# Score matmuls over 64 rows in two row groups instead of 32 rows in four

## The chip, the cores and the metric

The kernel runs on one core of a Trainium2 chip. Five engines work side by side and meet through semaphores: TensorE (PE, matrix products into PSUM), VectorE (DVE), ScalarE (ACT), GpSimd (POOL) and SyncE (SP, which issues the transfers). The metric is the time of one execution on the device in microseconds; less is better. Before the change two executions gave a median of 1937.16 us (1934.91 to 1939.40).

## The reference, cut to what matters

One sequence of 2048 tokens with 512 features passes through four blocks, each with a residual: multi-query softmax attention (A), linear attention (B), A again, B again, with the same weights. Block A has 32 heads of 16 features and one key and one value head that all share. `B_x` isn't used.

```python
def _A_ref(x, wq, wk, wv, wo):
    H = 32; Dh = D // H                       # 16
    q = (x @ wq).reshape(B, S, H, Dh).transpose(0, 2, 1, 3)
    k = x @ wk                                # (B, S, 16): one key for all heads
    v = x @ wv
    scores = jnp.einsum("bhqd,bkd->bhqk", q, k) * (Dh ** -0.5)
    p = softmax(scores)
    o = jnp.einsum("bhqk,bkd->bhqd", p, v)
    return o.transpose(0, 2, 1, 3).reshape(B, S, H * Dh) @ wo

def _B_ref(x, wqkv, wo):                      # linear attention, 32 heads of 16
    q, k, v = split_heads(x @ wqkv)
    pq, pk = phi(q), phi(k)                   # phi(t) = (t + 1 if t > 0 else exp(t)) + 1e-6
    kv = jnp.einsum("bhsd,bhse->bhde", pk, v); z = pk.sum(2)
    o = (pq @ kv) / (pq @ z + 1e-6)
    return merge_heads(o) @ wo

for layer in range(2):
    x = x + _A_ref(_layernorm(x), ...)
    x = x + _B_ref(_layernorm(x), ...)
```

Almost all the work is the softmax attention: per layer 32 heads x 2048 queries x 2048 keys, each with one exponential.

## The kernel before

**Units and positions.** A layer's attention is cut into 4 query blocks of 512 tokens (qb), 4 groups of 8 heads (g) and two halves of a group (par): 32 units. A unit holds 4 heads, called j, and goes over 16 tiles of 128 keys (kt): 64 positions (kt, j), in that order, with j running fastest (`Ctl.start`, L541 to L551). Two layers have 4096 positions.

**Scores.** `QT` holds the queries of a group with their 8 x 16 features on the 128 partitions. Four row groups of 32 partitions hold two heads each. Keys of 16 features are repeated on all partitions and kept in two masked copies, `Kr[:, 0]` and `Kr[:, 1]` (L486 to L496): copy par has zeros in the 16 rows of the other head of each pair. A position's scores are one matmul, keys against 512 queries, contracted over the 32 rows of row group j with copy par (`smm`, L572); the zeros take the second head out.

**Two ways from scores to weights.** PSUM has eight banks of 512 columns. Banks 0 to 2 and 3 to 5 are two sets: `fill` (L668) puts three positions into a set, and ACT exponentiates all 1536 columns in one instruction into one of the `PTA` buffers (L689). Bank 6 takes single positions for DVE, which works the exponential out in seven steps: L735 for each position, and L751 to L756 for two positions at once, into a `PTD` buffer (`dstep`, `dpass`). DVE's positions are taken `LEAD` = 26 ahead of ACT's. The same bank 6 serves all other products while attention runs: projections, transposes, residuals.

**PV.** For each position four matmuls (L608) multiply 128 queries' weights with `Vaug` (16 value columns and a column of ones) into 17 columns of bank 7, which collects a unit's 16 blocks of (query tile, head). After 64 positions DVE takes the reciprocals of the sums (L620) and writes the scaled result into `Osb` (L625); then the bank is free for the next unit. When both halves of a group are done, `epi_tr` (L793) transposes `Osb`, and after four groups `epi_y` applies `wo` and the residual (L809).

**Dense work beside attention.** When a query block of tokens is finished, its layer norm, the projections of linear attention (`b_prep`, `kv_block`, phi at L815 to L818) and their sums run beside the attention of the next blocks. So block 0 of a layer has little of it, blocks 1 to 3 have some 80 dense matmuls of 512 columns each. After the last block `b_main` runs the 16 tiles of linear attention (L889 to L931) and, in layer one, starts the layer norms and key projections of layer two (`a_ready`): this is the ramp, in which attention starts with one set.

**The order.** `Sched` plays the whole program through once, when the kernel is built, with a planned duration for each operation (`dur`), a priority and the state of buffers and banks. The order in which it starts operations on each engine is the order that is written out; semaphores carry the dependencies. The engines don't reorder at run time. `Ctl.step` decides in this play when a set is filled and when DVE takes a position. Planned durations of the score matmuls (L684, L734) don't depend on rows.

The softmax here doesn't subtract the row's maximum and nothing guards it: scores larger than these inputs give would overflow.

## Time and profile before

| | |
|---|---|
| median of two executions | 1937.16 us (1934.91 to 1939.40) |
| the profiled execution | 1937.57 us, span 1935.7 us |
| mean granted TensorE clock | 0.575 |
| busy: PE, DVE, ACT | 1778.2, 1712.9, 1702.0 us |
| score matmuls L572 | 4096 |
| PV matmuls L608 | 16384 |
| dense matmuls L475 | 704 |
| exponentials on ACT L689 | 1179 of up to three positions |
| positions on DVE L735 | 560 |

The profile's page gives the busy time of each engine, a row of 40 equal slices of the span with the granted clock of TensorE in tenths (5 is half, 9 is 90% or more), and groups of instructions: line, engine, operation, what it writes and reads, count, busy time and mean duration, then the idle time before them and what ended it. PEld are the weight loads, which overlap the matmuls. In rows by stretch, each number is the busy time of PE, PEld, DVE, ACT and POOL in that stretch with the number of instructions, then the granted clock, the share of the transfers and GB/s. In rows in order of time, the numbers are start and length in us. The ends of matmuls are modelled, so two starts say more than one length.

### The profile page before, as it was taken

To read this page: it belongs to the slowest core of one execution; us is meant where nothing else is said; L and a number is where in the kernel's file an instruction comes from. 1 tells how busy PE (TensorE), PEld (TensorE's weight loads), DVE (VectorE), ACT (ScalarE), POOL (GpSimd) and SP (SyncE) were. 2 spreads that over 40 slices of the span, in tenths; PEclk is the share of its full clock that TensorE was granted. 3 is DMA by queue.
4 is the path that set the end of the run, shared out by engine and by line. 5 is a ranking of instruction groups with operands and counts; after the bars stand their busy time and mean duration, and the time that the engine had idled before them with its cause. 6 is when DMAs were issued, how large, how long until landed. Compare 5 with 4: busy or idle time off the path is not lost.

```text
span 1935.7 us, 49030 instructions
## 1 busy us (share of the span) xinstructions
PE 1778.2 (92%) x22208; PEld 820.9 (42%) x22208; DVE 1712.9 (88%) x3063; ACT 1702.0 (88%) x1330; POOL 45.1 (2%) x77
## 2 busy tenths in 40 slices
PE   7999999999999999998889999999999999997977
PEld 4444444444444444443444444444444444443434
DVE  7899989999889988887879999899898989985977
ACT  6999999999989999997589999999998999986973
POOL 2000000000000000000100000000000000000000
PEclk8555556555665555555975555655565555556559
DMA  3000000000000000000000000000000000000001
GB/s 110 2 1 2 2 1 2 2 2 2 1 2 2 2 1 2 2 2 2 1 2 2 2 2 2 2 2 2 1 2 1 2 1 2 2 2 1 2 1 44
DMA packets 7808, 10.50 MB, mean 5 GB/s; under 512 B 1456, under 2 KB 7088, under 8 KB 7600
## 3 DMA queue, kind: packets, MB, share of 16 engines
q1 hardware_dynamic: 7600, 7.37, 1.2%
q8 instruction: 173, 2.83, 0.6%
q14 instruction: 35, 0.29, 0.0%
HBM read 5.28 MB, written 2.10 MB: 4 GB/s over the span
## 4 chain that ended last, share of the span: by engine, by line
PE 57%; DVE 29%; ACT 11%; issue 1%; DMA 0%; POOL 0%; SPq 0%
PE ps_all L572 27%; PE ps_all L608 16%; PE ps_all L475 11%; ACT PTA L689 10%; DVE xT L735 8%; DVE PTD L756 6%; DVE xu L751 3%; DVE xs L755 2%; DVE xs L752 2%; DVE xu L754 1%; DVE xs L753 1%; PE ps_all L920 1%; DVE stats L444 1%; PE ps_all L458 1%; DVE x_sb L931 1%
## 5 line engine op out<-in xcount | busy, mean ns | idle before, releaser
L689 ACT ACTIVATE PTA<-ps_all 128x1536 bf16<-128x1536 f32 x1179 | 1625.1, 1464 | 117.7 <-PE ps_all L572 108.8
L572 PE MATMUL ps_all<-QT,Kr 32*128 32x512 bf16 x4096 | 914.0, 582 | 80.0 <-ACT PTA L689 38.8
L608 PEld LDWEIGHTS ps_all<-Vaug,PTA 128*128 128x128 bf16 x14144 | 470.3, 104 | 566.0 <-issue 552.6
L608 PE MATMUL ps_all<-Vaug,PTA 128*128 128x17 bf16 x14144 | 584.0, 176 | 4.6 <-ACT PTA L689 2.5
L735 DVE TENSOR_SCALAR xT<-ps_all 128x512 int32<-128x512 f32 x560 | 385.1, 688 | 116.1 <-PE ps_all L572 105.1
L756 DVE SCALAR_TENSOR_TENSOR PTD<-xT,xs 128x1024 uint16<-128x1024 int32 x280 | 340.5, 1216 | 1.1
L572 PEld LDWEIGHTS ps_all<-QT,Kr 32*128 32x128 bf16 x4096 | 160.0, 98 | 311.6 <-ACT PTA L689 152.6
L751 DVE TENSOR_SCALAR xu<-xT 128x1024 f16<-128x1024 uint16 x280 | 192.3, 687 | 3.1
L755 DVE TENSOR_TENSOR xs<-xs,xu 128x1024 f16<-128x1024 f16 x280 | 191.0, 682 | 1.4
L752 DVE TENSOR_TENSOR xs<-xu 128x1024 f16<-128x1024 f16 x280 | 190.4, 680 | 0.5
L608 PE MATMUL ps_all<-Vaug,PTD 128*128 128x17 bf16 x2240 | 111.6, 176 | 16.6 <-DVE Osb L625 8.0
L753 DVE TENSOR_SCALAR xs<-xs 128x1024 f16<-128x1024 f16 x280 | 116.4, 416 | 1.0
L754 DVE TENSOR_SCALAR xu<-xu 128x1024 f16<-128x1024 f16 x280 | 117.0, 418 | 0.0
L608 PEld LDWEIGHTS ps_all<-Vaug,PTD 128*128 128x128 bf16 x2240 | 86.1, 104 | 66.8 <-DVE Osb L625 26.9
L475 PE MATMUL ps_all<-wqkv_sb,xnT 128*128 128x512 bf16 x256 | 106.3, 559 | 2.6 <-ACT xnT L464 1.4
L448 POOL TENSOR_TENSOR rstd<-veps,mhalf 128x1 f32<-128x1 f32 x64 | 40.9, 643 | 1842.2 <-DVE veps L446 1623.6
L815 ACT ACTIVATE e_buf<-ps_all 128x512 f32<-128x512 f32 x64 | 37.8, 597 | 39.8 <-PE ps_all L475 38.7
L475 PE MATMUL ps_all<-xnT,wq_sb 128*128 128x512 bf16 x128 | 55.8, 566 | 4.4 <-DVE xT L735 2.1
L475 PE MATMUL ps_all<-xnT,wqkv_sb 128*128 128x512 bf16 x128 | 52.4, 545 | 6.5 <-DVE pqT L818 5.6
L475 PE MATMUL ps_all<-wo_sb,OT 128*128 128x512 bf16 x128 | 51.9, 543 | 2.9 <-ACT OT L799 1.4
L444 DVE BATCH_NORM_STATS2 stats<-x_sb 128x6 f32<-128x512 bf16 x64 | 43.2, 683 | 3.5 <-DMA x_sb<-in_A_x_dram 3.3
L458 PE MATMUL ps_all<-ident,xn_buf 128*128 128x128 bf16 x256 | 31.2, 267 | 15.3 <-DVE xn_buf L451 13.6
(64 smaller groups left out, 625.9 us busy)
## 6 DMA issues: line engine op xcount, KB each, us to landing
out_dram<-x_sb SPq DMA_DIRECT2D x16, 128.0 KB, 1.7
x_sb<-in_A_x_dram SPq DMA_DIRECT2D x3, 512.0 KB, 7.3
wqkv_sb<-in_B_wqkv_dram SPq DMA_DIRECT2D x1, 1536.0 KB, 11.3
x_sb<-in_A_x_dram SPq DMA_DIRECT2D x2, 256.0 KB, 3.5
wq_sb<-in_A_wq_dram SPq DMA_DIRECT2D x1, 512.0 KB, 5.5
wo_sb<-in_A_wo_dram SPq DMA_DIRECT2D x1, 512.0 KB, 8.5
wo_sb<-in_B_wo_dram SPq DMA_DIRECT2D x1, 512.0 KB, 10.9
wk_sb<-in_A_wk_dram SPq DMA_DIRECT2D x1, 16.0 KB, 2.7
```

Source lines behind the costliest of these rows:

```text
L444: add(DV, tdv(512), lambda e: e.bn_stats(stats[:, t, 0:6], x_sb[:, t, :]), reads=[("x", t)], writes=[("st", t)], prio=prio, name="bn")
L475: i = e.matmul(bank(h.idx, n), lhsT=l, rhs=r, start=(c + k == 0), stop=(c + k == len(mms) - 1))
L572: return e.matmul(bank(b), lhsT=Kr[32 * j:32 * j + 32, par, kt * P:(kt + 1) * P], rhs=QT[32 * j:32 * j + 32, qb % 2, g, :], start=True, st ...
L608: i = e.matmul(bank(7, 17, (qs * 4 + j) * 17), lhsT=src(qs), rhs=Vaug[:, kt, 0:17], start=(first and qs == 0), stop=(qs == 3), skip_group_ ...
L689: oe = add(AC, tac(m * 512), lambda e: e.activation(PTA[:, hp.idx, 0:m * 512], bank(3 * s, m * 512), ACTF.Exp, scale=SCALE), deps=[o] + pr ...
L735: o = add(DV, tdv(512), lambda e: e.tensor_scalar(out=xT[:, hx.idx, i * 512:(i + 1) * 512], in0=bank(6), scalar1=SCALE * LOG2E * 65536.0, ...
L751: o = add(DV, tdv(1024, 0.52), lambda e: e.tensor_scalar(out=u_, in0=lo, scalar1=1.0 / 65536, scalar2=-0.5, op0=ALU.mult, op1=ALU.add), de ...
L752: o1 = add(DV, tdv(1024, 0.52), lambda e: e.tensor_tensor(out=s_, in0=u_, in1=u_, op=ALU.mult), deps=[o] + c["prev"], name="xsq", **kw)
L753: o2 = add(DV, tdv(1024, 0.26), lambda e: e.tensor_scalar(out=s_, in0=s_, scalar1=XK, scalar2=-XW, op0=ALU.mult, op1=ALU.add), deps=[o1], ...
L754: o3 = add(DV, tdv(1024, 0.26), lambda e: e.tensor_scalar(out=u_, in0=u_, scalar1=1.0, scalar2=XL, op0=ALU.mult, op1=ALU.add), deps=[o1], ...
L755: o4 = add(DV, tdv(1024, 0.52), lambda e: e.tensor_tensor(out=s_, in0=s_, in1=u_, op=ALU.mult), deps=[o2, o3], name="xc", **kw)
L756: o5 = add(DV, tdv(1024), lambda e: e.scalar_tensor_tensor(out=PTD[:, hp.idx, :].bitcast(U16), in0=xT[:, k, :], scalar=2.0 ** -9, in1=s_, ...
```

## The change

A position's scores are contracted over 64 rows instead of 32. `RG` = 64 makes `NRG` = 2 row groups of 64 partitions, each with four heads, and `NM` = 4 masked copies of the keys, each with one head of four left in. Position j of half par uses row group j % 2 and copy 2 par + j // 2. So a unit still has four heads, but other ones: the columns of bank 7 and the write into `Osb` are ordered accordingly, and `Osb` is laid out as [group, query tile, 128].

To make room for the copies, buffers are fewer: `PTA` and `PTD` 5 instead of 6, `e_buf` 2 instead of 3, and `Osb2`, `OT2`, `rdenB` 2 instead of 3. DVE may work on a single position at the end of a layer, where it took only pairs. A hook adds dummy matmuls where PE is idle in the plan, with a factor `DUMMY` = 0.0, which issues none; its zero tile is set once by POOL.

```diff
+    RG = 64
+    NRG, NM = P // RG, RG // DH
+    DUMMY = 0.0
...
-    NXN, NE = 3, 3
+    NXN, NE = 3, 2
...
-    mpar = sb("mpar", [P, 2], FP32)
+    mpar = sb("mpar", [P, NM], FP32)
...
-    Kr = sb("Kr", [P, 2, S], BF16)
+    Kr = sb("Kr", [P, NM, S], BF16)
...
-    NPA, NPD, NDX = 6, 6, 2
+    NPA, NPD, NDX = 5, 5, 2
...
-    Osb = sb("Osb", [P, 2, 4, D], BF16)
+    Osb = sb("Osb", [P, 2, NG, 4, P], BF16)
...
-    NO2 = 3
+    NO2 = 2
...
+    zer = sb("zer", [P, 240], BF16)
+    add(PO, 0.3, lambda e: e.memset(zer[:], 0.0), writes=["zer"], prio=4)
...
-        for m in range(2):
+        for m in range(NM):
             def ev(e, m=m):
...
-            ops[m] = add((DV, AC), ..., deps=[o] + ([ops[0]] if m else []), uses=[h], rel=[h] if m else [],
+            ops[m] = add((DV, AC), ..., deps=[o] + ([ops[m - 1]] if m else []), uses=[h], rel=[h] if m == NM - 1 else [],
...
-            return e.matmul(bank(b), lhsT=Kr[32 * j:32 * j + 32, par, kt * P:(kt + 1) * P],
-                            rhs=QT[32 * j:32 * j + 32, qb % 2, g, :], start=True, stop=True)
+            i, m = (j % NRG, par * (4 // NRG) + j // NRG)
+            r = slice(i * RG, (i + 1) * RG)
+            return e.matmul(bank(b), lhsT=Kr[r, m, kt * P:(kt + 1) * P], rhs=QT[r, qb % 2, g, :], start=True, stop=True)
...
-                    i = e.matmul(bank(7, 17, (qs * 4 + j) * 17), lhsT=src(qs), rhs=Vaug[:, kt, 0:17],
+                    i = e.matmul(bank(7, 17, (qs * 4 + (j % NRG) * (4 // NRG) + j // NRG) * 17), lhsT=src(qs), rhs=Vaug[:, kt, 0:17],
...
-            ov_ = Osb[:, qb % 2, :, 128 * g:128 * (g + 1)].rearrange("p s (j r d) -> p s j r d", j=4, r=2)[:, :, :, par, :]
+            HP = 4 // NRG
+            ov_ = Osb[:, qb % 2, g, :, :].rearrange("p s (i x) -> p (s i) x", i=NRG)[:, :, par * HP * DH:(par + 1) * HP * DH].rearrange("p a (m d) -> p a m d", d=DH)
...
             if self.pa >= n:
                 self.tail = True
-                self.layer_done()
+                if self.dcur is not None:
+                    self.dpass(self.dcur)
+                    self.dcur = None
+                    return True
                 return False
...
+            w = 512 * len(c["pos"])
...
+    def idle(now):
+        if ctl.layer is None or ctl.ramp or ctl.tail or DUMMY <= 0:
+            credit[0], credit[1] = 0.0, now
+            return
...
-                i = e.transpose(v[:, qs, :], Osb[:, qb % 2, qs, g * P:(g + 1) * P], ident[:])
+                i = e.transpose(v[:, qs, :], Osb[:, qb % 2, g, qs, :], ident[:])
```

## The prediction

> **What bounds the kernel now.** I read the page's busy times and clock row first, then the busy time by stage, then the order of instructions inside one stage, then short stretches of the clock.

> ```profile
> PE 1778.2 (92%) x22208; PEld 820.9 (42%) x22208; DVE 1712.9 (88%) x3063; ACT 1702.0 (88%) x1330; POOL 45.1 (2%) x77
> ...
> PEclk8555556555665555555975555655565555556559
> ...
> L689 ACT ACTIVATE PTA<-ps_all 128x1536 bf16<-128x1536 f32 x1179 | 1625.1, 1464 | 117.7 <-PE ps_all L572 108.8
> L572 PE MATMUL ps_all<-QT,Kr 32*128 32x512 bf16 x4096 | 914.0, 582 | 80.0 <-ACT PTA L689 38.8
> ```

> Three engines are near full and TensorE runs at half its clock nearly everywhere. ACT needs 1625.1 / 1179 = 1.378 us for a set of three positions. By stage (busy time of each engine, granted clock):

> ```profile
> 57.00:240.00 183.00, 170.13 (x2265) 78.49 (x2262) 173.55 (x293) 175.10 (x128) 0.00 (x0) 0.50 0.01 2
> 240.00:908.00 668.00, 629.83 (x8033) 286.39 (x8030) 600.14 (x1038) 616.64 (x464) 11.07 (x12) 0.55 0.01 2
> ...
> 1000.00:1191.00 191.00, 175.22 (x2311) 80.97 (x2310) 179.13 (x302) 179.66 (x132) 0.00 (x0) 0.51 0.01 2
> 1191.00:1876.00 685.00, 637.40 (x8028) 287.86 (x8028) 598.80 (x1039) 618.24 (x463) 7.88 (x12) 0.54 0.01 2
> ```

> The first row is query block 0 of layer one: seven units (of 64 positions) end in it, 26.1 us each, and ACT (175 of 183) and DVE (174) bind. The second is blocks 1 to 3, 24 units of 27.8 us: PE (630 of 668) is fuller than ACT (617) and DVE (600). Layer two repeats this.

> Inside block 0, at clock 0.50 (start, length, engine, line):

> ```profile
> 200.42 1.03 PE L572 MATMUL ps_all<-QT,Kr 32*128 32x512 bf16 x4
> 201.38 0.49 PE L608 MATMUL ps_all<-Vaug,PTA 128*128 128x17 bf16 x12
> 201.80 0.61 PE L572 MATMUL ps_all<-QT,Kr 32*128 32x512 bf16 x3
> 202.34 0.49 PE L608 MATMUL ps_all<-Vaug,PTA 128*128 128x17 bf16 x12
> ```

> Three scores in three row groups start together and cost one pass: 0.54 us from 201.80 to 202.34. A fourth whose row group is taken costs a second pass: 0.96 us (200.42 to 201.38). The difference, 0.42 us, is also the step of dense matmuls (four of 512 columns in a row take 1.89 us, one 0.61: 0.427 each, 1200 columns per us).

> **What moves the clock.** The records of the clock change only every 3.413 us. The dense matmuls of L475 in four such stretches (busy and count, then PEld, then clock):

> ```profile
> 116.32:119.73 3.41, 0.00 (x0) 0.00 (x0) 0.50 0.00 0
> ...
> 256.27:259.68 3.41, 1.66 (x4) 0.30 (x2) 0.50 0.00 0
> 259.68:263.09 3.41, 0.42 (x2) 0.21 (x3) 1.00 0.02 5
> 263.09:266.51 3.42, 1.09 (x3) 0.15 (x1) 0.50 0.00 0
> ```

> The same view for L572 and L608 counts 7 scores and 23 PVs in the second row, 7 and 36 in the third. I weigh each matmul's columns by the share of 128 rows that it uses: dense 512, score 512 x 32/128 = 128, PV 17. Row two sums to 2048 + 896 + 391 = 3335, and the next stretch runs at 1.00; row three to 1024 + 896 + 612 = 2532, and the next falls back to 0.50. I counted every stretch so, spreading matmuls over their streaming time: of 482 at 0.50, the 33 followed by 1.00 all hold 3040 or more, the other 449 at most 3061. From 1.00 the border is nearly the same (falls up to 3030, once 3231; stays from 3020). Other weights for a score separate worse. So **a stretch of about 3050 weighted columns buys the next one at full clock.** TensorE was busy for all of 116.32 to 119.73, at 0.50.

> [...]

> **The change, part by part.** Durations are of the profiled execution: 1937.6 us, span 1935.7 and 1.9 around it, 0.4 over the median.

> *Scores.* With two row groups, three positions give groups like 0, 1, 0: two passes. A 64-row pair does not occur in the trace. Bounds: still one pass, 0.54 us, by the x3 row; all one after another, like the 128-row matmuls, 0.54 + 2 x 0.427 = 1.39. I take two passes, 0.97, nearest to the x4 row. The score's weight doubles to 256 (bounds: 128 and 512).

> PE per unit now: 560 of 4096 positions go to DVE, so a unit has 8.75 of those and 18.4 sets. Sets 18.4 x (0.54 + 0.42) = 17.7; DVE's positions 8.75 x (0.36 score, between 0 and 0.54, + 0.107 PV) = 4.1; dense work, transposes and gaps 1.6: 23.4 of the 26.1 in block 0. Blocks 1 to 3 have 10 dense matmuls per unit, 4.3, and 1.7 more around them: 27.8, which is the measured pace. The account closes.

> After, at half clock: a set is 0.97 + 0.42 = 1.39, no longer below ACT's 1.378, before anything else is added. 18.4 x 0.427 = +7.9 per unit, and -0.5 because a DVE score beside a set finds a free group one time in two instead of one in four. **Block 0: 30.9; blocks 1 to 3: 35.2.** At full clock a pass is half as long, 0.213; three scores start 0.32 us before their PVs (299.06 to 299.38), twelve PVs take 0.32 to 0.39, so a set costs PE 0.32 + 0.21 + 0.35 = 0.88, and 1.05 with its share of DVE scores, so ACT binds at 18.4 x 1.378 + 0.6 = 26; I take 26.7, near block 0's pace.

> *The clock after.* A set with its share of DVE positions weighs 3.47 x (256 + 68) = 1126. Half clock, PE full: 1126 in 1.6 us, 2400 in a stretch. Only dense work lifts it: a dense column displaces 0.58 of such a column, so 1550 dense columns (three matmuls) are wanted. Full clock, at ACT's pace: 64 x 324 / 26.7 x 3.413 = 2650 plus dense, so 400 keep it open. In block 0, 2 to 6 in 100 stretches hold 1550, nine in ten less than 400: half clock. In blocks 1 to 3, 20 to 23 in 100 hold 1550, some 17 at the slower pace; half hold less than 400, and with the spread of the rest some 42 in 100 fall. The first stretch after a rise is an exception: PE, which had kept ACT waiting, can do 3.41 / 1.05 = 3.2 sets in it against ACT's 2.5 and fills both bank sets, 0.7 x 1126 = 790 more, so I let it hold always. A rise is then waited for 1 / 0.17 = 5.9 stretches and lasts 1 + 1 / 0.42 = 3.4: share of full clock 3.4 / 9.3 = 0.37. Pace: 1 / (0.37/26.7 + 0.63/35.2) = 31.5 us.

> *Sum.* Blocks 1 to 3: 48 x (31.5 - 27.8) = +178. Block 0: 8 x 4.8 + 8 x 4.3 = +73 (26.6 in layer two).

> *K copies.* Two more evictions for each of 16 projections, 32 x 0.48 = 15 us on DVE and ACT in the ramps. Between 0 and 15; I take +8: in the first 50 us both engines have 12 us idle.

> *Buffers.* No wait of ACT or DVE for PVs (L608) stands among the waits over 1.7 us in total but that of the normalization, so five of PTA and PTD are taken as free; if not, ACT stops behind PE, which the half-clock pace holds already. NE two: bank 6 allows one phi at a time in attention. NO2 two: a tile of the last linear stage holds its buffer some 3.7 us (L898 at 1903.76 to L920 at 1906.75 and its end), 1.85 per tile against 1.8 now: +1, at most 5. The zero memset lies on idle POOL; the dummies are off; the new order inside PSUM and Osb moves the same elements. Odd batches at the end save at most one DVE round, 2 us.

> Total 1937.6 + 178 + 73 + 8 = 2197; less 10 for half the chance that the order written out loses the hole at 1750 to 1767, where all waits for the next QT: **2187 us**.

> **Rivals.**
> *Half clock throughout* (chance 0.09). It holds if dense work rarely fills a stretch once PE is saturated. 48 x 7.4 + 73 + 8 = +436: 2375.
> *Blocks 1 to 3 stay at full clock* (0.14). For it: at 26.7 their mean is 2650 + 750 = 3400, above 3050. Against it: half their stretches hold next to no dense work. 48 x (26.7 - 27.8) = -53, +73, +8: 1965.
> *Faster: full clock in all attention* (0.11). Scores alone must hold the gate: at block 0's 26.1 us the weight is 2710 plus 100 dense, 8% short. If 64 rows weigh 8% more than half, it locks open. Then PE never binds: -53, block 0 -5, hole -17, K +8: 1870.
> *It doesn't do what it says* (0.04): 64-row matmuls don't pair. A third pass, 64 x 7.9 us more: above 2700.
> The forecast has 0.62, by itself 2080 to 2310. The range takes in the third case and stops before the fast and the slowest ones: 1950 to 2335. Two per cent, 39 us, is about what a measurement here can tell from no change. Faster 0.11; same 0.07 (half of the 1965 case); slower 0.82.

> **What will show it.** L572 with 64 rows; x3 groups 0.96 us to the PV at 0.50 and 0.54 at 1.00; ACT's wait for L572 up from 109 us to several hundred; block 0 near 31 us per unit at 0.50 to 0.55; blocks 1 to 3 with clock 0.6 to 0.7; ACT's 1464 ns unchanged. Wrong would make it: a clock above 0.8 in block 0, or x3 groups that stay at 0.54 at half clock.

## The result, and the profile after

The changed kernel takes 2108.86 us (median of two executions, 2108.28 to 2109.45) against 1937.16 us before: a ratio of 1.0886, 95% interval 1.0831 to 1.0942. It is slower by 172 us, on the side and inside the range that were forecast, 78 us less than the forecast. Its profiled execution took 2108.28 us, span 2106.6. In its code the score matmul stands at L580, ACT's exponential at L699, PV at L615, the dense matmuls at L481 and DVE's first step at L750.

From the page after (busy times, clock in 40 slices, the two groups):

```profile
PE 2000.5 (95%) x22208; PEld 842.0 (40%) x22208; DVE 1719.4 (82%) x3073; ACT 1731.7 (82%) x1347; POOL 48.0 (2%) x78
...
PEclk8555556656767679755797555666768787689759
...
L699 ACT ACTIVATE PTA<-ps_all 128x1536 bf16<-128x1536 f32 (+1 forms) x1182 | 1653.1, 1464 | 268.5 <-PE ps_all L580 263.2
L580 PE MATMUL ps_all<-QT,Kr 64*128 64x512 bf16 x4096 | 1194.4, 521 | 46.2 <-ACT PTA L699 26.5
```

ACT does the same work in the same 1464 ns, but waits 263 us for scores instead of 109. PE's scores grew from 914 to 1194 us, although their mean fell from 582 to 521 ns: one score reads 0.61 us at half clock and 0.39 at full (medians), and the clock is now above half in most slices of blocks 1 to 3. Busy time by stage after (PE, PEld, DVE, ACT, POOL, then the granted clock):

```profile
68.00:281.00 213.00, 212.16 (x2259) 84.36 (x2256) 175.34 (x294) 178.29 (x126) 0.00 (x0) 0.52 0.01 2
281.00:1019.00 738.00, 713.64 (x8035) 294.25 (x8033) 594.73 (x1029) 627.14 (x466) 10.26 (x12) 0.68 0.01 1
...
1122.00:1336.00 214.00, 210.16 (x2275) 84.59 (x2273) 178.62 (x299) 180.19 (x128) 0.00 (x0) 0.56 0.01 1
1336.00:2045.00 709.00, 680.46 (x8031) 288.95 (x8030) 597.83 (x1040) 621.55 (x464) 11.54 (x12) 0.73 0.01 2
```

The stages are cut at the same units as before. In block 0 PE is busy for 212 of 213 us and binds; ACT has dropped from 175 of 183 to 178 of 213. The 170.9 us by which the span grew, by the ends of units: the ramp of layer one 10.7, its block 0 30.3 (seven units of 30.5 instead of 26.1), its blocks 1 to 3 70.3 (30.8 instead of 27.8 per unit), the linear stage and ramp between the layers 6.0, block 0 of layer two 27.7, its blocks 1 to 3 23.7 (29.5 instead of 28.6, in which the hole of 20 us before is gone), the tail 2.2.

Scores and PVs in order of time, first from block 0 at half clock, then from a stretch at full clock:

```profile
202.57 1.03 PE L580 MATMUL ps_all<-QT,Kr 64*128 64x512 bf16 x3
203.54 0.49 PE L615 MATMUL ps_all<-Vaug,PTA 128*128 128x17 bf16 x12
203.96 1.03 PE L580 MATMUL ps_all<-QT,Kr 64*128 64x512 bf16 x3
204.92 0.49 PE L615 MATMUL ps_all<-Vaug,PTA 128*128 128x17 bf16 x12
...
403.08 0.60 PE L580 MATMUL ps_all<-QT,Kr 64*128 64x512 bf16 x3
403.61 0.46 PE L615 MATMUL ps_all<-Vaug,PTA 128*128 128x17 bf16 x12
```

Three scores now hold PE for 0.97 us before their PVs can start (202.57 to 203.54), where it was 0.54; at full clock it is 0.53. In the single instructions behind these merged rows, two of the three start together and the third 0.40 us later (0.22 at full clock).

### The profile page after: what moved, and what is told of

Same layout as the page of the kernel before. It is cut to its first block, busy times and chain, and to the rows that moved or that the text cites. A ratio compares the mean times of both kernels' runs of the same rounds, so it can differ in the third digit from the quotient of the medians.

```text
span 2106.6 us, 49073 instructions
## 1 busy us (share of the span) xinstructions
PE 2000.5 (95%) x22208; PEld 842.0 (40%) x22208; DVE 1719.4 (82%) x3073; ACT 1731.7 (82%) x1347; POOL 48.0 (2%) x78
## 4 chain that ended last, share of the span: by engine, by line
PE 70%; DVE 17%; ACT 12%; issue 1%; DMA 0%; POOL 0%; SPq 0%
PE ps_all L580 41%; PE ps_all L615 18%; ACT PTA L699 11%; PE ps_all L481 8%; DVE xT L750 3%; DVE PTD L772 3%; DVE xs L771 1%; DVE xu L767 1%; DVE xs L768 1%; PE ps_all L949 1%; DVE xs L769 1%; DVE xu L770 1%; PE ps_all L822 1%; DVE stats L450 1%; PE ps_all L464 0%
## 5 line engine op out<-in xcount | busy, mean ns | idle before, releaser
L699 ACT ACTIVATE PTA<-ps_all 128x1536 bf16<-128x1536 f32 (+1 forms) x1182 | 1653.1, 1464 | 268.5 <-PE ps_all L580 263.2
L580 PE MATMUL ps_all<-QT,Kr 64*128 64x512 bf16 x4096 | 1194.4, 521 | 46.2 <-ACT PTA L699 26.5
L615 PEld LDWEIGHTS ps_all<-Vaug,PTA 128*128 128x128 bf16 x14152 | 465.9, 102 | 757.9 <-issue 741.9
L615 PE MATMUL ps_all<-Vaug,PTA 128*128 128x17 bf16 x14152 | 583.6, 175 | 3.5 <-DVE Osb L632 2.8
L750 DVE TENSOR_SCALAR xT<-ps_all 128x512 int32<-128x512 f32 x558 | 384.2, 688 | 242.9 <-PE ps_all L580 238.5
L580 PEld LDWEIGHTS ps_all<-QT,Kr 64*128 64x128 bf16 x4096 | 197.8, 101 | 287.2 <-ACT PTA L699 108.1
L615 PE MATMUL ps_all<-Vaug,PTD 128*128 128x17 bf16 x2232 | 111.2, 175 | 10.5 <-DVE PTD L772 5.0
L615 PEld LDWEIGHTS ps_all<-Vaug,PTD 128*128 128x128 bf16 x2232 | 84.2, 102 | 68.1 <-issue 28.8
L481 PE MATMUL ps_all<-wqkv_sb,xnT 128*128 128x512 bf16 x256 | 90.4, 485 | 2.7 <-ACT xnT L470 1.4
L844 ACT ACTIVATE e_buf<-ps_all 128x512 f32<-128x512 f32 x64 | 39.1, 614 | 28.9 <-PE ps_all L481 24.6
L481 PE MATMUL ps_all<-xnT,wq_sb 128*128 128x512 bf16 x128 | 49.8, 508 | 1.2 <-DVE Kr L496 0.3
L481 PE MATMUL ps_all<-wo_sb,OT 128*128 128x512 bf16 x128 | 49.5, 531 | 1.4 <-ACT OT L828 1.4
L481 PE MATMUL ps_all<-xnT,wqkv_sb 128*128 128x512 bf16 x128 | 46.2, 491 | 1.2 <-DVE xT L750 1.1
L845 DVE TENSOR_SCALAR e_buf<-e_buf 128x512 f32<-128x512 f32 x64 | 26.8, 419 | 22.7 <-ACT e_buf L844 22.5
```

Of the source, the lines that this page charges most:

```text
L481: i = e.matmul(bank(h.idx, n), lhsT=l, rhs=r, start=(c + k == 0), stop=(c + k == len(mms) - 1))
L580: return e.matmul(bank(b), lhsT=Kr[r, m, kt * P:(kt + 1) * P], rhs=QT[r, qb % 2, g, :], start=True, stop=True)
L615: i = e.matmul(bank(7, 17, (qs * 4 + (j % NRG) * (4 // NRG) + j // NRG) * 17), lhsT=src(qs), rhs=Vaug[:, kt, 0:17], start=(first and qs == ...
L699: oe = add(AC, tac(m * 512), lambda e: e.activation(PTA[:, hp.idx, 0:m * 512], bank(3 * s, m * 512), ACTF.Exp, scale=SCALE), deps=[o] + pr ...
L750: o = add(DV, tdv(512), lambda e: e.tensor_scalar(out=xT[:, hx.idx, i * 512:(i + 1) * 512], in0=bank(6), scalar1=SCALE * LOG2E * 65536.0, ...
```

## The experiments

The theory: a set costs a second pass over the array, and the clock, taken to go by columns weighted with rows as counted in this kernel's stretches, gives a part of it back. The first rival puts the loss on the other edits; others let the clock follow how long the array is busy. "The gate" in the recorded texts is the step between half and full clock. Four kernels ran on one chip, beside its own runs of the kernel before (median 1945.6 us), and a fifth later on another, where the kernel before took 1939.2 us.

**All other edits, four row groups kept.**

```diff
-    RG = 64
+    RG = 32
```

> The changed kernel with RG = 32: two copies of K and four row groups as before, but all its other edits (five PTA and PTD buffers, two e_buf and Osb2, odd batches, the new layout of Osb, the zero tile). Theory (passes and clock explain the whole loss): within 25 us of the kernel before, 1915 to 1960, clock 0.57 to 0.59, three scores 0.54 us before their PVs. Rival (the smaller buffers or the new order cost a good part of the 172 us): 2000 or more.

Measured: 1946.8 us, ratio 1.0006 (0.9993 to 1.0018), clock 0.567. By stage, cut at the same units, its first layer is that of the kernel before:

```profile
55.00:238.00 183.00, 169.93 (x2266) 78.56 (x2264) 173.51 (x292) 175.10 (x128) 0.00 (x0) 0.50 0.01 2
238.00:906.00 668.00, 630.11 (x8032) 286.51 (x8033) 600.38 (x1038) 616.37 (x464) 11.13 (x12) 0.55 0.01 2
```

The smaller buffers, the odd batches, the new layouts and the zero tile together cost nothing that can be measured. The whole 172 us belong to the 64 rows and the two more copies that they need.

**The second pass without the weight.** A head's keys fill 16 rows of the 64, the other 48 are zeros, so the contraction can be cut to the 32 rows in which the head lies.

```diff
-            r = slice(i * RG, (i + 1) * RG)
+            r = slice(i * RG + 32 * (m // 2), i * RG + 32 * (m // 2) + 32)
```

> The changed kernel, but each score matmul contracts only those 32 of its 64 rows in which its head lies (the other 32 rows of the copy are zeros): a unit then still uses only two places in the array, two passes per set, but a score weighs 128 as before, not 256. Theory (the clock goes by weighted columns, and the clock's gain pays back a part of the second pass): attention stays at half clock, 0.50 to 0.53 in blocks 1 to 3, units of 31 us in block 0 and 35 us after it, 2109 + 48 x (35.3 - 30.2) = 2340, between 2290 and 2380. Rival (the clock follows how long the array is busy): clock and time as in the changed kernel, 2109.

Measured: 2285.43 us, ratio 1.1743 (1.1720 to 1.1767). By stage, cut at the same units:

```profile
68.00:278.00 210.00, 209.33 (x2259) 83.26 (x2256) 174.79 (x293) 178.45 (x126) 0.00 (x0) 0.50 0.01 2
278.00:1091.00 813.00, 806.09 (x8033) 303.39 (x8033) 598.51 (x1030) 641.68 (x466) 10.27 (x12) 0.50 0.01 1
```

The clock never leaves 0.50 in attention, and PE is busy for 806 of 813 us. The order of instructions, the counts and the passes are those of the changed kernel; only the rows named in 4096 matmuls differ, and those left out are zeros in K. So the second pass, with some 25 us that lie in the ramps, the middle and the tail, costs 17%, and the weight of the rows brings half of it back: 2285 to 2109. That the array was busier (806 of 813 us) did not raise the clock. The stretch of the kernel before on which the prediction rests says the same: TensorE is busy for all of it and of the next one (PE, the first number after the length), and the clock stays at 0.50:

```profile
116.32:119.73 3.41, 3.41 (x43) 1.40 (x40) 3.31 (x6) 3.41 (x4) 0.00 (x0) 0.50 0.00 0
119.73:123.15 3.42, 3.42 (x47) 1.67 (x46) 3.11 (x7) 3.28 (x3) 0.00 (x0) 0.50 0.00 0
```

The time is 55 us below the expected 2340 (its terms, 2109 + 48 x 5.1, make 2354), because a unit of blocks 1 to 3 takes 33.8 us and not 35.3.

**All 128 rows.** Eight masked copies; room for them comes from keeping 8 instead of 16 tiles of the linear block's keys and values.

```diff
-    RG = 64
+    RG = 128
...
-    pk_tok = sb("pk_tok", [P, T, D], BF16)
+    pk_tok = sb("pk_tok", [P, 8, D], BF16)
...
-    vaugB = sb("vaugB", [P, T, H * 17], BF16)
+    vaugB = sb("vaugB", [P, 8, H * 17], BF16)
...
-            phi(h, o, pk_tok[:, t, :], ("pk", t), 2.2)
+            phi(h, o, pk_tok[:, t % 8, :], ("pk", t % 8), 2.2)
```

(and `t % 8` likewise where `vaugB` is written and both are read)

> The changed kernel with RG = 128: eight masked copies of K, each score contracts all 128 rows, so three scores of a set always take three passes, and a score weighs 512. To make room, pk_tok and vaugB keep 8 tiles instead of 16. Theory: even at half clock PE brings (3.47 x 580 = 2015) per 2.07 us, 3320 in a stretch, over the border of some 3060, so attention opens the gate by itself and keeps it open: clock above 0.95 throughout, three scores 0.75 us before their PVs, PE 1.25 us per set against ACT's 1.378 in block 0, about 1.46 with dense work; block 0 25.5 us per unit, blocks 1 to 3 26 to 27.3; 48 more evictions per layer of K cost 10 to 20: 1890, between 1840 and 1950. Rival (a third pass costs as the second did, the gate doesn't open by rows): half clock, 43 us per unit, above 2500.

Measured: 1830.61 us, ratio 0.9403 (0.9387 to 0.9419): faster than both kernels, by 6% and, by the two ratios, 14%. By stage:

```profile
64.00:237.00 173.00, 158.64 (x2263) 94.40 (x2261) 171.87 (x296) 171.31 (x127) 0.00 (x0) 1.00 0.01 2
237.00:856.00 619.00, 580.01 (x8031) 345.22 (x8031) 587.57 (x1032) 610.34 (x465) 8.67 (x12) 1.00 0.01 2
```

The clock is 1.00 through attention, and with a third pass PE is still less full (580 of 619) than ACT (610). Units take 24.7 us in block 0 and 25.8 after it. The rival that a further pass only costs more is out. It came out 60 us under the expected value. One reason is in the order of time:

```profile
302.46 0.81 PE L580 MATMUL ps_all<-QT,Kr 128*128 128x512 bf16 x3
303.11 0.45 PE L615 MATMUL ps_all<-Vaug,PTA 128*128 128x17 bf16 x12
...
305.02 0.45 PE L615 MATMUL ps_all<-Vaug,PTA 128*128 128x17 bf16 x12
305.32 0.25 PE L615 MATMUL ps_all<-Vaug,PTD 128*128 128x17 bf16 x4
305.43 0.81 PE L580 MATMUL ps_all<-QT,Kr 128*128 128x512 bf16 x3
```

From scores to PVs are 0.65 us, three steps of 0.216 and hardly more, where 0.75 was expected (dense matmuls of 512 columns start 0.216 us apart at full clock, median in the profile after). With 64 rows at full clock it is 0.53, two steps and 0.10. Four PVs before scores take 0.11 us (305.32 to 305.43), with 64 rows at full clock 0.19 (median of 61). So in these rows the way from scores over row groups to PVs over all rows took some 0.1 us beyond the steps, and the way back 0.08 more than with 128 rows, which show neither.

The waits of the weight loads differ in the same way, with 64 rows (first row) and with 128 (in all, number, longest):

```profile
PEld ps_all L615 <- issue: 770.7, 1254, 0.8
PEld ps_all L615 <- issue: 2.6, 10, 0.3
```

With 64 rows the first weight load of the PVs starts together with the PVs (403.61 us), when the scores have passed; with 128 it starts under the last score (302.89, with the PVs at 303.11). A load takes about 0.1 us (102 ns on the page after), so these runs don't tell a price of the change itself from a load that nothing hides.

Over 32 rows in distinct row groups the scores run side by side here, three in one pass, 0.54 us at half clock; padded with zeros to 128 rows, one after another, 0.65 us at full clock, the same scores make the faster kernel, 1831 us against 1947, with the clock in attention at 1.00 instead of 0.50 to 0.55.

**Weight without a second pass.** 32 rows again, and 3020 dummy matmuls on zeros.

```diff
-    RG = 64
+    RG = 32
...
-    DUMMY = 0.0
+    DUMMY = 0.3
```

> The changed kernel with RG = 32 and DUMMY = 0.3: one pass per set as before, and 3020 matmuls of 128 rows by 240 zero columns (47 per unit) between the rest; their sums add zero. They weigh 240 each if zeros count. Theory: at full clock block 0 holds 1752 x 26.1/25.2 + 1530 = 3340 per stretch and stays open in 8 of 10 stretches, blocks 1 to 3 nearly always; at half clock 2590 and 2730, so a rise waits for dense work; clock about 0.65 in block 0, 0.85 to 0.95 in blocks 1 to 3; 1905, between 1850 and 1980. Rival (zeros don't count, or the gate follows busy time): half clock with 0.2 us more per dummy, 33 and 37 us per unit, 2400 or more.

Measured: 2052 to 2073 us, ratio 1.0589 (1.0537 to 1.0642): between theory and rival, and outside both ranges.

```profile
55.00:268.00 213.00, 206.03 (x2640) 105.81 (x2640) 172.95 (x290) 178.12 (x128) 0.00 (x0) 0.70 0.01 2
268.00:980.00 712.00, 687.09 (x9140) 354.61 (x9136) 588.80 (x1025) 624.36 (x465) 10.28 (x12) 0.78 0.01 2
```

Zeros count here: the clock rises from 0.50 to 0.70 in block 0, and every one of 66 rises follows a stretch of some 3000 or more, dummies weighed with 240. But full clock holds worse than I had reckoned: in blocks 1 to 3 one stretch in five falls, where nearly none was expected to. A stretch at full clock there holds 3900 on average, with a spread of 1000: the dummies stand where the plan has PE idle, so they come in bunches (none to 23 in a stretch, 6.6 on average). And at half clock they make a full PE fuller: 5.6 to 5.8 scores per stretch in blocks 1 to 3 against 6.4 in the half-clock experiment above.

**The changed kernel with dummies.**

```diff
-    DUMMY = 0.0
+    DUMMY = 0.06
```

> The changed kernel with DUMMY = 0.06: 964 matmuls of 128 rows by 240 zero columns (15 per unit), which add zero, on top of the scores over 64 rows. Theory (weight per stretch rules): at full clock a stretch holds some 500 more, so fewer fall (0.18 instead of 0.33), at half clock each dummy costs the saturated PE 0.2 us, 3 us per unit; share of full clock in blocks 1 to 3 about 0.6, pace 1 / (0.62/25.4 + 0.38/36.8) = 28.8 against 30.2 in the changed kernel; block 0 nearly as it is, 30.9. Together 2050, between 2000 and 2110. Rival (dummies only fill time in which PE waits, and lock the gate open): 1900 or less.

Measured: 2070.63 us, ratio 1.0639 (1.0576 to 1.0701) against its own runs of before, clock 0.788. In the expected range, 2.5 points better than without dummies and far from a clock that stays at full. The share of full clock in blocks 1 to 3 was 0.69 and 0.59. The gain isn't even, though. The first and the third row are block 0 of layer one and of layer two, the others blocks 1 to 3:

```profile
59.00:265.00 206.00, 200.65 (x2364) 84.56 (x2364) 174.49 (x295) 175.69 (x127) 0.00 (x0) 0.70 0.01 2
265.00:958.00 693.00, 669.93 (x8402) 300.71 (x8402) 595.45 (x1037) 619.99 (x464) 10.36 (x12) 0.84 0.01 2
1063.00:1290.00 227.00, 222.47 (x2385) 87.96 (x2383) 177.42 (x296) 181.55 (x129) 0.00 (x0) 0.61 0.01 2
1290.00:2009.00 719.00, 695.09 (x8404) 300.37 (x8401) 593.83 (x1033) 621.74 (x464) 10.53 (x12) 0.79 0.01 2
```

In the profiled executions (here 2076 us, the longest of four) layer one gains: 29.4 us per unit in block 0 and 28.9 after it, where it was 30.5 and 30.8 without dummies. Layer two loses: 32.4 and 30.0, with one unit of 42, where it was 30.5 and 29.5, although its clock is higher too. Why isn't shown.

## Why the prediction was right, and where its sum was off

*The second pass*: right, 0.97 us at half clock and 0.53 at full. *The weight of 64 rows*: right. I counted the stretches of the changed kernel as before: of 386 at half clock, the 56 followed by full clock hold 3057 or more, the others at most 3073. That is about three quarters of the 4096 columns that pass in 3.413 us at half clock, at 1200 per us. Weights of 0.45 or 0.55 of a column for a score mix the two sides a little more than 0.5 does; the 0.25 of 32 rows mixes them far more.

*Block 0*: right, 30.5 us per unit against 30.9, clock 0.52 and 0.56 where 0.50 to 0.55 was expected. *Ramps, K copies, the linear stage*: 18.9 us measured in the ramps, the middle and the tail; the sum had 17 for them (8 for K and one unit of block 0 per layer).

*Blocks 1 to 3*: mis-sized, and nearly the whole error is there: 94 us measured, 168 forecast (178 less 10 for the hole), 74 of the 78 us. Their terms:

| term | forecast | measured, layer one and two |
|---|---|---|
| pace at full clock | 26.7 us per unit | 25.1, 25.0 (8.70, 8.73 scores per stretch) |
| pace at half clock | 35.2 | 35.6, 35.3 (6.14, 6.18 scores per stretch) |
| chance of a rise per half-clock stretch | 0.17 | 0.18, 0.21 |
| chance of a fall in the first stretch, later | 0, 0.42 | 0.12 and 0.04, 0.38 and 0.33 |
| share of full clock | 0.37 | 0.37, 0.45 |
| us per unit | 31.5 | 30.8, 29.5 |

The step that failed by most is "I take 26.7, near block 0's pace". I had worked out ACT's bound, 26, and then added a margin from a block in which PE was already 93% busy; at full clock ACT simply runs at its bound, here 1.37 us per set. With 25.1 in its place the same line gives 30.6, and with the measured 35.6 for half clock too it gives 30.8, layer one's value; over 48 units that is 34 us. Layer two stood more often at full clock, 0.45, and took 29.5 us per unit: another 30 us or so over its 24 units. And its hole went entirely, 20 us instead of the 10 that I had given for a chance of one half: no unit there takes over 36 us, where one took 47.

*The account of PE*: it closed for the wrong reason, and its 35.2 came near the measured value by luck. It said that PE fills all of the 27.8 us of a unit in blocks 1 to 3. In the half-clock experiment PE is really full, and the second pass and the rest come to 33.8, not 35.2. Before the change, PE was idle for 38 of 668 us there, 1.6 per unit, nearly the "1.7 more around them"; in the half-clock experiment it is idle for 7 of 813. So idle time was counted as work that PE would still have to do. In the changed kernel's own half-clock stretches this doesn't show, since they hold fewer scores than those of the experiment, 6.1 and 6.2 against 6.4. A part of that is the choice of stretches: those before a rise, in layer one, hold 3.7 dense matmuls of 512 columns and 4.0 scores, the other half-clock stretches 0.4 and 6.6. But on average they hold 1.00 dense matmuls in layer one and 1.11 in layer two, against 0.94 in the experiment, which is too little for the whole difference; the rest stays open.

*Rivals*: half clock throughout is what the second experiment made by hand, 2285 instead of the 2375 that I gave it. Full clock in all attention failed where the prediction put it: in block 0 the weight at ACT's pace stays below the border, and half the weight for 64 rows is exact enough that the missing 8% weren't there. With 128 rows they are. Full clock in blocks 1 to 3 held for 0.37 and 0.45 of the stretches, not for all. A third pass is out: two of the three scores start together.

## What to carry to other kernels

Look at the granted clock by stage before you count TensorE's time: here scores over 32 rows ran side by side, three in one pass, and the kernel still took 1947 us where scores over 128 rows, one after another, took 1831, with the clock in attention at 1.00 and not at 0.50 to 0.55. Reckon what each 3.4 us stretch holds in columns weighted with rows, at half clock with PE full and at full clock at the other engines' pace: in these runs only the version with 128 rows, which by this reckoning passes the border of some 3050 found here in both states, stayed at full clock (1.00), and the one between (64 rows) paid for the passes and got the clock for a part of the time. Work with zeros that adds rows was worth more here than packing. Dummies beside a full PE brought no kernel below the one before: they took 2.5 points off the loss with 64 rows and added 6 points with 32.
